# A gated causal convolution on one core: oct 0's eight direct tiles made as four pairs with a shared sum

## The chip, the cores and the metric

The kernel runs on one core of one Trainium2 chip. The time is the device time of one execution in microseconds (us); the profile's span lies inside it. The engines are TensorE (PE in the profile; its weight loads are PEld), VectorE (DVE), ScalarE (ACT), GpSimd (POOL) and the queue engine SyncE (SP), which issues nearly all DMAs.

## The reference

A dilated causal convolution over time, 15 taps at distance 2, with 144 channels in and 288 out, then a gate and a projection. All data are bf16; x is 2 x 16000 x 144.

```python
xp = jnp.pad(x, ((0, 0), (28, 0), (0, 0)))              # (K-1)*dil = 28
h = sum(einsum('btc,cd->btd', xp[:, 28-2*i : 28-2*i+T], w[i]) for i in range(15))
z = tanh(h[..., :144]) * sigmoid(h[..., 144:])
return z @ w_o
```

## The kernel before

**Tiles.** The 32000 time steps lie as 128 partitions of 250 consecutive steps. A tile is one position within these 250, on all 128 partitions: 128 rows that one matmul multiplies by a tap's weights. Eight positions make an oct; 250 = 2 + 31 x 8. The octs -4 to -1 hold the 28 steps of history and the two odd positions, oct 0 the first eight, and octs 1 to 30 the rest, handled in 15 pairs of octs. Of the 144 input channels the first 128 are transposed into XA (by channel), and the last 16 are gathered for eight taps at a time into XBc, copied to STB and transposed into XB. So the straightforward sum for a tile is 15 matmuls of XA with the taps WA and two of XB with WB. All these matmuls are recorded under one line (740, the helper `mm`), each 128x128 by 128x288.

**Direct tiles.** The first ten output positions, the two odd ones (k = 0, 1) and oct 0 (k = 2 to 9), are made in this straightforward way by `direct` (taps, in four pieces of weights as these arrive, the last first) and `direct_b` (the two of XB). Two tiles share a pair of PSUM banks, `dp`, and `finish` passes both through tanh and sigmoid (ACT, lines 761 and 764) and the product (DVE, line 769) into Z. In the planner they are floating: they have low priority and fill PE where nothing else can run.

**The loop.** From oct 1 on, a faster algorithm makes tiles in groups from sums of taps and differences of tiles. Its 30 units u = 0 to 29 (two for each pair of octs) run in steps t = -1 to 29. DVE makes the differences ahead (line 692): V and DU between tiles two and four apart, DD of V, and GX, GU, GV and GD between octs (`v_first`, `v_second`, `v_third`, `g_diffs`). Sums of weights (line 623, `wsum`) go to WS (neighbouring taps), WC, WT, WV and WD. PE forms parts of the results in PSUM: the items S0, S1, X0a to X1b, Y0a, Y0b, Y01, VE and VF. ACT copies a half-made bank to its neighbour (`copy`, line 898; 925 and 967 for whole pairs), and DVE adds the parts (lines 1019, 1031, 1040). The items D00 to D11 put the last matmuls in, and `finish` follows. O0 to O2 are projections: SP transposes Z into ZT, PE multiplies it by WOR (line 839), ACT copies PSUM to OS (line 847), SP stores it.

**Order.** A string in PATTERNS gives the order of the items for each t, with PATTERN where there is no entry. A + after an item means that it is done for the next unit. `stage(m)` prepares a pair of octs: load Xr, copy its 128 channels to STA and transpose to XA (`load_xa`), gather the others with `compact_chunk` into XBc, difference them (line 639), copy twice to STB (`load_xb`, line 672) and transpose to XB. `prepare(m)` makes the differences. SPREAD and SPREAS say at which step of two t's the ten pieces of `prepare` and the eight of `stage` may start: by a soft dependence on PE's last loop matmul before it.

**The planner.** Nothing of this is a fixed program order. `_Graph` records operations with what they read and write, a modelled duration and a priority, and `run` fills each engine's list: always the operation that can start first by the model, then the one of lower priority number, then the one recorded first. Combining, gates and copies in PSUM have 0, weight sums and evictions 1, differences 2, direct tiles 2. The two XB transposes by PE stand behind an empty `warm(0)`, which wants bank 6, in which oct 0's XA is transposed. The engines then run these lists in order, with semaphores between.

**The start.** Four loads of x (Xp) and four of weights (WA, last taps first) come in. PE warms up with 40 matmuls on ONES (line 548), transposes octs -4 to 0 (line 572), and DVE (oct -4) and ACT (the others, line 581) evict them to XA. ACT also compacts the 16 channels (line 541), and XB for octs -1 and 0 is transposed by PE (line 609) and evicted by ACT (line 613). The first loads through staging are those of octs 1 and 2. POOL loads WOR in 16 DMAs (line 1146), which wait until XB of oct 2 has landed (`xb2`).

Of the kernel before, what the change touches and what calls it, by code (L numbers as in the profile page):

```python
# [5 lines left out]
ACT = mybir.ActivationFunctionType  # L6
# [5 lines left out]
NP = 128  # L12
# [315 lines left out]
def _conv_wavenet_kernel(nc, x, w, w_o, out):  # L328
# [38 lines left out]
    KF = 0  # L367
    WARMS = 0
    LAG = 2
    PATTERNS = {29: 'O2 O1 Y01 Y0a D11 O0 Y0b D01 D00 D10', 28: 'Y0a X0a+ O1+ Y0b X0b+ O2+ D11 S0+ D10 X1a+ D00 Y01 S1+ X1b+ VE+ O0+ D01 VF+', 1: 'Y0a O2+ X0a+ Y0b X0b+ D11 X1a+ O1+ D00 S0+ D10 Y01 S1+ X1b+ D01 VE+ VF+ O0+', 0: 'Y0a X0a+ Y0b D11 X0b+ D00 X1a+ O2+ O1+ O0+ S0+ D10 Y01 S1+ X1b+ D01 VE+ VF+', 2: 'Y0a O2+ X0a+ O1+ Y0b X0b+ D11 D00 S0+ X1a+ D10 Y01 S1+ X1b+ D01 VE+ O0+ VF+'}  # L370
    EARLY = 4
    EARLYC = 1
    SPREAD = 12
    SPREAS = 9
    PATTERN = "Y0a O2+ X0a+ O1+ Y0b X0b+ D11 D00 S0+ X1a+ D10 Y01 S1+ X1b+ D01 VE+ VF+ O0+"

    with contextlib.ExitStack() as st:
        def sb(name, shape, dt):
            return st.enter_context(nc.sbuf_tensor(name, shape, dt))
# [5 lines left out]
        STB = sb("STB", [NP, NST, 12, 128], BF16)  # L385
        XA = sb("XA", [NP, NA, 8, 128], BF16)
        V = sb("V", [NP, NV, 2, 4, 128], BF16)
        DU = sb("DU", [NP, ND, 4, 128], BF16)
        DD = sb("DD", [NP, ND, 2, 4, 128], BF16)
        XB = sb("XB", [NP, NB, 12, 128], BF16)  # L390
# [50 lines left out]
        def aslot(o):  # L441
            return (o + 4) % NA
# [10 lines left out]
        def oct_of(e):  # L453
            return (e - E0) // 8, (e - E0) % 8
# [90 lines left out]

        def warm(n):
            bk = _Bank(BANK_O)
            g.add("pe", [lambda t: t.matmul(PS[:, BANK_O * 512:BANK_O * 512 + 128], lhsT=ID[:], rhs=ONES[:], start=True, stop=True)] * n,  # L548
                  r=["ID", "ONES"], alloc=[bk], frees=[bk], dur=0.07 * n)

        warm(40)
# [94 lines left out]
        def load_xa(o):  # L646
            s, q = aslot(o), o % NST
            ci = chunk_of(8 * o)
            i0 = 8 * o - CH[ci][0]
            src = Xr[:, ci % NX, i0:i0 + 8, 0:DA]  # L650
            if o <= EARLY:
                g.add("act", lambda a: a.activation(STA[:, q, :, :], src, ACT.Copy), r=[("Xr", ci % NX)], w=[("STA", q)], dur=0.92, prio=1, soft=gate[:1])
            else:
                g.add("dve", lambda v: v.tensor_copy(STA[:, q, :, :], src), r=[("Xr", ci % NX)], w=[("STA", q)], dur=0.335, prio=2, soft=gate[:1])
            g.add("sp", lambda e: e.dma_start_transpose(XA[:, s, :, :], STA[:, q, :, :].rearrange("p a b -> p (a b)")),
                  r=[("STA", q)], w=[("XA", s)], dur=1.3, dma="xa", nbytes=8 * 128 * 128 * 2)

        def load_xb(o, parts=(0, 1)):
            s, q = bslot(o), o % NST
            e0 = E0 + 8 * o  # L660
            ck = set()
            for e in range(e0 - 28, e0 + 8):
                if e >= EP:
                    ck.update([("XBc", chunk_of(e - E0)), ("XBd", chunk_of(e - E0))])
                else:
                    ck.update(hk5 + ["XBcz", "XBd_h"])
            m4 = (e0 + 2) // 4

            for h in parts:
                def cp(v, h=h):  # L670
                    src = bass.AP(XBc[:].tensor, (MB - 1 - m4 - h) * DB, [[8 * MB * DB, NP], [MB * DB, 6], [1, 128]])
                    return v.activation(STB[:, q, 6 * h:6 * h + 6, :], src, ACT.Copy)  # L672
                g.add("act", cp, r=sorted(ck, key=str), w=[("STB", q, h)], dur=0.708, prio=2 if gate else 0, soft=gate[:1])
            if 1 not in parts:
                return
            return g.add("sp", lambda e: e.dma_start_transpose(XB[:, s, :, :], STB[:, q, :, :].rearrange("p a b -> p (a b)")),
                  r=[("STB", q, 0), ("STB", q, 1)], w=[("XB", s)], dur=1.7, dma="xb", nbytes=12 * 128 * 128 * 2)
# [13 lines left out]
        def tt(dst, a, b, r, wk, n, prio=2):  # L691
            return g.add("dve", lambda v: v.tensor_tensor(dst, a, b, ALU.subtract), r=r, w=wk, dur=t_tt(n), prio=prio, soft=gate[:1])

        V0 = -3

        def v_first(o):
            s, p, q = aslot(o), aslot(o - 1), vslot(o)
            if o == V0:
                for f, pos in ((0, 6), (1, 2)):
                    tt(ap(V, 8 * q + 4 * f + 2, [2]), ap(XA, 8 * s + pos, [2]), ap(XA, 8 * s + 4, [2]), [("XA", s)], [("V", q, f)], 256)  # L700
                return
            ka = [("XA", s), ("XA", p)]
            if p == s - 1:
# [361 lines left out]
        def direct(k, b, pi, t0, t1, after=None):  # L1065
            e = H + k
            g.add("pe", region(b, [(lambda e_=e - DIL * i: xa_tile(e_)) for i in range(t0, t1)], [(lambda i_=i: WA[:, i_, :]) for i in range(t0, t1)], t0 == 12),
                  r=[("XA", aslot(o)) for o in sorted(set(oct_of(e - DIL * i)[0] for i in range(t0, t1)))] + [("WA", pi)], dur=(t1 - t0) * MM, floating=k >= KF, prio=2 if k >= KF else 1, soft=(after,), **({"alloc": [b.bk]} if t0 == 12 and k % 2 == 0 else {"w": [b.bk]}))

        def direct_b(k, b):  # L1070
            e = H + k
# [10 lines left out]
            return ((-1) % NZ, 6 + k) if k < 2 else (0, k - 2)  # L1082

        wa_order = [(3, wa_pieces[3]), (2, wa_pieces[2]), (1, wa_pieces[1]), (0, wa_pieces[0])]
        for pi, (t0, t1) in wa_order:
            for k in range(6):
                direct(k, db[k], pi, t0, t1)
        fin = []
        for k in range(6):
            direct_b(k, db[k])  # L1090
            if k % 2:
                fin.append(finish(dp[k // 2], zdir(k - 1), zdir(k)))

        def direct_parts(k):
            out = [lambda pi=pi, t0=t0, t1=t1: direct(k, db[k], pi, t0, t1, fin[0] if k >= 8 and t0 == 12 else xb_op if k == 6 and t0 == 12 else None) for pi, (t0, t1) in wa_order]

            def last():
                direct_b(k, db[k])
                if k % 2:
                    finish(dp[k // 2], zdir(k - 1), zdir(k))  # L1100
            return out + [last]

        for k in range(6, 10):
            for f in direct_parts(k):
                f()
        load_xa(1)
        compact_chunk(0)
        g.add("act", lambda a: a.activation(WC[:, 2, 3, :], WB[:, 1, :], ACT.Copy, scale=-1.0), r=[("WB", 1)], w=[("WB", 3)], dur=0.31, prio=2)
# [5 lines left out]
        for i in range(4):  # L1114
# [3 lines left out]
            else:  # L1118
                wsum(lambda: WC[:, 1, 3, :], lambda: WA[:, 12, :], lambda: WA[:, 14, :], [("WA", 3)], [("WC", 1, 3)], 0.25)
                wsum(lambda: WC[:, 0, 3, :], lambda: WC[:, 1, 3, :], lambda: WA[:, 13, :], [("WC", 1, 3), ("WA", 3)], [("WC", 0, 3)], 0.25)  # L1120
        for i in range(4):
            n = 2 if i < 3 else 1
            wsum(lambda i=i, n=n: WS[:, 2 * i:2 * i + n, :], lambda i=i, n=n: bass.AP(WA[:].tensor, 4 * i * N2, [[15 * N2, NP], [2 * N2, n], [1, N2]]),
                 lambda i=i, n=n: bass.AP(WA[:].tensor, (4 * i + 1) * N2, [[15 * N2, NP], [2 * N2, n], [1, N2]]), [("WA", i)], [("WS", i)], 0.4 if n == 2 else 0.25)
        wsum(lambda: WB[:, 2, :], lambda: WB[:, 0, :], lambda: WB[:, 1, :], [("WB", 0), ("WB", 1)], [("WB", 2)], 0.25)
        wsum(lambda: WT[:, 0:2, :], lambda: bass.AP(WC[:].tensor, 0, [[12 * N2, NP], [2 * N2, 2], [1, N2]]), lambda: bass.AP(WC[:].tensor, N2, [[12 * N2, NP], [2 * N2, 2], [1, N2]]),
             [("WC", 0, i) for i in range(4)], [("WT", 0), ("WT", 1)], 0.4)
# [4 lines left out]
        for h in range(2):  # L1132
            wsum(lambda h=h: WD[:, h, :, :], lambda h=h: WA[:, 8 * h:8 * h + 3, :], lambda h=h: WA[:, 8 * h + 4:8 * h + 7, :], wak, [("WD", h)], 0.52)
        wsum(lambda: WT[:, 5, :], lambda: WS[:, 5, :], lambda: WA[:, 14, :], [("WS", i) for i in range(4)] + [("WA", 3)], [("WT", 5)], 0.25)
        for o in range(-3, 1):
            v_first(o)
        for o in range(-2, 1):
            v_second(o)
        for o in range(-2, 1):
# [194 lines left out]
```

## Time and profile before

| | |
|---|---|
| median of 6 runs | 322.39 us (321.72 to 324.72) |
| profiled execution | 322.66 us, its span 320.9 us |
| PE busy, matmuls | 313.9 us, 2670 |
| DVE / ACT / POOL busy | 282.2 / 269.1 / 16.9 us |
| DMA | 50.40 MB, mean 157 GB/s |
| granted TensorE clock | 1.000 |

Stretches of the span, in us from its start. "Idle" is the stretch less the engine's busy time.

| stretch | what it is | PE busy | DVE busy | ACT busy |
|---|---|---|---|---|
| 0 to 8.9 | loads, warm-up, first XA | 6.83 | 1.84 | 3.21 |
| 8.9 to 16.3 | XA of octs -2 to 0, direct tiles | 7.37 | 6.56 | 5.53 |
| 16.3 to 24.9 | direct tiles; weight sums on DVE | 8.60 | 8.60 | 8.60 |
| 24.9 to 32.9 | t = -1, with direct tiles | 8.00 | 8.00 | 6.35 |
| 32.9 to 43.9 | t = 0, with the last direct tiles | 11.00 | 9.56 | 9.33 |
| 43.9 to 62.6 | t = 1 and 2 | 18.64 | 17.80 | 16.23 |
| 62.6 to 287.2 | t = 3 to 26, each 9.36 | 224.60 | 209.55 | 197.02 |
| 287.2 to 297.0 | t = 27 | 9.80 | 5.59 | 8.03 |
| 297.0 to 321.0 | t = 28, 29 and the rest | 19.05 | 14.70 | 14.85 |

How to read it: the page's first part gives each engine's busy time and share of the span. The chain that ended last goes back from the last instruction to what released it, so it names the work that set the end; in time order its columns are start, duration, engine and line. A row of the timeline has start, duration from first start to last end, engine, line, operation, tiles (out <- in), count, and in brackets the idle time before it with its releaser. An instruction's own duration has a tail that overlaps the next one, so the cost of one more instruction in a full engine is the distance between starts: matmuls last 286 ns each and start some 123 ns apart.

### The profile page before, as it was taken

Reading aid. Unit: us, or ns where it says so; the run is one execution under the profiler, and the core shown is the slowest. Engines: PE = TensorE matmul, PEld = TensorE weight load, DVE = VectorE, ACT = ScalarE, POOL = GpSimd, SP = SyncE. Lnnn points to the kernel's source line nnn. Section 1 sums busy time; section 2 is a strip of 40 time slices with the busy share of each in tenths; the row PEclk is TensorE's granted clock in tenths of the full one; section 3 lists DMA queues with packets and bytes.
Section 4 is the critical chain, followed back from the end, with each engine's and each line's share of the span. In section 5 each row is a group of like instructions: output and inputs, shape, how many; then the busy total and the mean of one; then the engine's idle time right before and its main releaser. Section 6 shows DMA issues by size and latency. Waiting matters only on the chain.

```text
span 320.9 us, 6963 instructions
## 1 busy us (share of the span) xinstructions
PE 313.9 (98%) x2670; PEld 244.1 (76%) x2670; DVE 282.2 (88%) x610; ACT 269.1 (84%) x636; POOL 16.9 (5%) x29
## 2 busy tenths in 40 slices
PE   7999999999999999999999999999999999999994
PEld 7787777777777777777777777777777777777674
DVE  1899989898998989899898989989898998884774
ACT  2798689889797988979798897979889797778674
POOL 8108100000000000000000000000000000000000
PEclk9999999999999999999999999999999999999999
DMA  8799994949589396969969499893969377131753
GB/s 207 213 219 186 233 217 99 195 111 202 153 144 243 76 236 108 179 176 102 243 119 235 109 196 158 134 254 73 181 167 191 90 142 172 47 68 72 112 128 96
DMA packets 127822, 50.40 MB, mean 157 GB/s; under 512 B 119134, under 2 KB 121615, under 8 KB 127789
## 3 DMA queue, kind: packets, MB, share of 16 engines
q1 hardware_dynamic: 127273, 49.62, 75.7%
q0 software_dynamic: 512, 0.33, 0.8%
q8 instruction: 21, 0.34, 0.4%
q14 instruction: 12, 0.10, 0.1%
q10 hardware_dynamic: 4, 0.01, 0.0%
HBM read 11.82 MB, written 9.22 MB: 66 GB/s over the span
## 4 chain that ended last, share of the span: by engine, by line
PE 96%; ACT 2%; DVE 1%; issue 0%; POOL 0%; ACTq 0%; POOLq 0%
PE PS L740 84%; PE PS L839 9%; PE PS L548 1%; PE PS L572 1%; ACT TS L761 0%; PE PS L870 0%; PE PS L797 0%; ACT PS L898 0%; ACT TS L764 0%; DVE WC L623 0%; ACT OS L847 0%; ACT OS L801 0%; PE PS L609 0%; PE PS L789 0%; ACT PS L925 0%
## 5 line engine op out<-in xcount | busy, mean ns | idle before, releaser
L1019 DVE TENSOR_TENSOR Xp<-PS,UX 128x576 f32<-128x576 f32 x90 | 62.8, 750 | 19.6 <-PE PS L740 19.3
L740 PE MATMUL PS<-WB,XB 128*128 128x288 bf16 x260 | 71.9, 286 | 0.0
L1031 DVE TENSOR_TENSOR PS<-PS,Xp 128x576 f32<-128x576 f32 x90 | 68.2, 757 | 2.1 <-ACT OS L847 1.0
L740 PE MATMUL PS<-WA,GD 128*128 128x288 bf16 x360 | 69.9, 286 | 0.0
L761 ACT ACTIVATE TS<-PS 128x288 f16<-128x288 f32 x125 | 51.5, 412 | 11.9 <-PE PS L740 10.8
L847 ACT ACTIVATE OS<-PS 128x432 bf16<-128x432 f32 (+1 forms) x88 | 42.3, 488 | 13.8 <-PE PS L839 12.8
L764 ACT ACTIVATE TS<-PS 128x288 f16<-128x288 f32 x125 | 51.5, 412 | 0.0
L672 ACT ACTIVATE STB<-XBc 128x768 bf16<-128x768 bf16 x60 | 50.7, 854 | 0.7 <-DMA XB<-STB 0.7
L898 ACT ACTIVATE PS<-PS 128x288 f32<-128x288 f32 x120 | 46.3, 408 | 2.6 <-PE PS L740 2.5
L967 ACT ACTIVATE UX<-PS 128x576 f32<-128x576 f32 x60 | 39.2, 653 | 10.4 <-PE PS L740 10.1
L740 PE MATMUL PS<-WS,GU 128*128 128x288 bf16 x210 | 44.3, 287 | 0.0
L839 PE MATMUL PS<-WOR,ZT 128*128 128x144 bf16 (+1 forms) x322 | 42.4, 253 | 0.0
L740 PEld LDWEIGHTS PS<-WA,GD 128*128 128x128 bf16 x360 | 34.6, 98 | 9.6 <-DVE PS L1031 0.8
L769 DVE TENSOR_TENSOR Z<-TS 128x288 bf16<-128x288 f16 x125 | 36.7, 298 | 4.3 <-ACT TS L764 4.0
L740 PE MATMUL PS<-WC,XB 128*128 128x288 bf16 x120 | 34.3, 286 | 0.0
L839 PEld LDWEIGHTS PS<-WOR,ZT 128*128 128x128 bf16 x322 | 27.9, 98 | 6.3 <-ACT OS L847 0.5
L740 PE MATMUL PS<-WD,DD 128*128 128x288 bf16 x180 | 31.9, 286 | 0.5 <-ACT PS L898 0.5
L740 PE MATMUL PS<-WC,V 128*128 128x288 bf16 x180 | 30.6, 286 | 0.0
L740 PE MATMUL PS<-WA,DD 128*128 128x288 bf16 x180 | 30.6, 286 | 0.0
L740 PEld LDWEIGHTS PS<-WB,XB 128*128 128x128 bf16 x260 | 25.4, 98 | 6.4
L740 PE MATMUL PS<-WT,DU 128*128 128x288 bf16 x120 | 24.5, 286 | 0.1
L740 PEld LDWEIGHTS PS<-WS,GU 128*128 128x128 bf16 x210 | 18.5, 98 | 7.5 <-ACT PS L898 0.3
(82 smaller groups left out, 469.3 us busy)
## 6 DMA issues: line engine op xcount, KB each, us to landing
Xr<-in_x_dram SPq DMA_DIRECT2D x15, 576.0 KB, 4.6
out_dram<-OS SPq DMA_DIRECT2D x30, 288.0 KB, 3.2
WA<-in_w_dram SPq DMA_DIRECT2D x3, 288.0 KB, 5.7
ZT<-Z SPq DMA_TRANSPOSE x32, 3.7
Xp<-in_x_dram SPq DMA_DIRECT2D x2, 252.0 KB, 5.8
XA<-STA SPq DMA_TRANSPOSE x30, 3.4
XB<-STB SPq DMA_TRANSPOSE x30, 5.0
Xp<-in_x_dram SPq DMA_DIRECT2D x1, 441.0 KB, 4.3
```

The source lines that it names most:

```text
L548: g.add("pe", [lambda t: t.matmul(PS[:, BANK_O * 512:BANK_O * 512 + 128], lhsT=ID[:], rhs=ONES[:], start=True, stop=True)] * n, r=["ID", " ...
L672: return v.activation(STB[:, q, 6 * h:6 * h + 6, :], src, ACT.Copy)
L740: return lambda t: t.matmul(bank(bk.b), lhsT=lhs(), rhs=rhs(), start=start, stop=True, skip_group_check=True)
L761: return a.activation(TS[:, s, 0, :, :], both(bk, 0, D), ACT.Tanh)
L764: return a.activation(TS[:, s, 1, :, :], both(bk, D, D), ACT.Sigmoid)
L769: return v.tensor_tensor(dst, TS[:, s, 0, :, :], TS[:, s, 1, :, :], ALU.mult)
L839: return t.matmul(PS[:, c0:c0 + n * D], lhsT=ZT[:, zt, blk, :], rhs=WOR[:, wi:wi + n, :].rearrange("p a b -> p (a b)"), start=first, stop= ...
L847: return e.tensor_copy(dst, src) if eng == "dve" else e.activation(dst, src, ACT.Copy)
L898: g.add("act", lambda e: e.activation(bank(bk.b + 1), bank(bk.b), ACT.Copy), w=[bk], dur=t_act(N2), prio=0)
L967: g.add("act", lambda e: e.activation(UX[:, k, u % NU, :, :], both(X, 0, N2), ACT.Copy), r=[X], w=[("UX", k, u % NU)], frees=[X], dur=t_ac ...
L1019: g.add("dve", lambda v, k=k, wi=wi, vb=vb, us=us: v.tensor_tensor(wslot(wi), both(vb, 0, N2), UX[:, k, us, :, :], ALU.add), r=[vb, ("UX", ...
L1031: return v.tensor_tensor(both(d, 0, N2), src, wslot(wi), ALU.add)
```

## The change

Oct 0's eight tiles are now made as four pairs. A pair is two positions two steps apart: a tile e with weights of all taps, and the tile e + 2. Written with neighbouring taps (2j, 2j+1), both tiles contain the same term, the sum of these two taps' weights (WS) times one tile of XA, and each has a remainder: a difference of two tiles two apart (V) times one of the two taps. So PE first makes the shared sum in the pair's first bank (`pair_sum`, eight matmuls), ACT copies it to the second bank, and then PE adds the remainders to both (`pair_own`, 15 matmuls for the two banks together), and the XB tail and `finish` as before (`pair_end`). The tiles k = 0 and 1 stay direct. Since the own matmuls add on to what ACT wrote, the second banks are written by a matmul first: `warm` goes over the odd banks with 12 of its 40 matmuls (128, 128 and 32 columns in each), and for the third pair, whose banks served the transposes, one extra matmul does it.

The differences V now begin one oct earlier: oct -3 gets the whole set and a small VX serves for oct -4. The sums WS and the first differences are recorded ahead of the direct tiles, not behind all weight sums. The sums of the first NQ0 = 2 pairs are mixed with the two direct tiles; the others come later.

The copies to STB for octs 3 and 4 (two each) go from ACT to DVE (BDVE); the copies to STA for octs 1 to 4 stay on ACT (AACT names the same octs as EARLY did). The compaction of chunk 1 goes from ACT to DVE (EARLYC 1 to 0). The patterns of t = 0, 1 and 2 are written anew, t = -1 and 27 get one of their own, and SPREAD goes from 12 to 10.

```diff
-    PATTERNS = {..., 1: 'Y0a O2+ X0a+ Y0b X0b+ D11 X1a+ O1+ D00 S0+ D10 Y01 S1+ X1b+ D01 VE+ VF+ O0+', 0: 'Y0a X0a+ Y0b D11 X0b+ D00 X1a+ O2+ O1+ O0+ S0+ D10 Y01 S1+ X1b+ D01 VE+ VF+', 2: 'Y0a O2+ X0a+ O1+ Y0b X0b+ D11 D00 S0+ X1a+ D10 Y01 S1+ X1b+ D01 VE+ O0+ VF+'}
-    EARLY = 4
-    EARLYC = 1
-    SPREAD = 12
+    PATTERNS = {..., 1: 'X0a+ Y0a O1+ O2+ Y0b X0b+ D11 X1a+ D00 S0+ O0+ X1b+ Y01 S1+ D10 D01 VE+ VF+', 0: 'Y0a X0a+ Y0b X0b+ D11 D00 S0+ D10 O2+ O1+ Y01 S1+ X1a+ D01 VE+ X1b+ VF+ O0+', 2: 'Y0a O0+ X0a+ O1+ Y0b X0b+ D11 D00 X1a+ S0+ D10 Y01 S1+ X1b+ D01 VE+ VF+ O2+', -1: 'X0a+ Y0a Y01 O2+ Y0b S0+ D11 D10 X0b+ O1+ X1a+ S1+ X1b+ D01 VE+ D00 O0+ VF+', 27: 'Y0a O2+ X0a+ O1+ Y0b X0b+ D11 D00 S0+ X1a+ D10 Y01 S1+ X1b+ D01 VE+ O0+ VF+'}
+    AACT = (1, 2, 3, 4)
+    BDVE = (3, 4)
+    EARLYC = 0
+    NQ0 = 2
+    NQD = 0
+    SPREAD = 10
     PATTERN = "Y0a O2+ X0a+ O1+ Y0b X0b+ D11 D00 S0+ X1a+ D10 Y01 S1+ X1b+ D01 VE+ VF+ O0+"
...
+        VX = sb("VX", [NP, 2, 128], BF16)
...
+            fns = [lambda t, c=512 * b + c, m=min(128, N2 - c), first=c == 0: t.matmul(PS[:, c:c + m], lhsT=ID[:], rhs=ONES[:, 0:m], start=first, ...)
+                   for b in (1, 3, 5, 7) for c in range(0, N2, 128)] if n else []
+            fns += [lambda t: t.matmul(PS[:, BANK_O * 512:BANK_O * 512 + 128], lhsT=ID[:], rhs=ONES[:], start=True, stop=True)] * max(0, n - 12)
...
-                g.add("act", cp, r=sorted(ck, key=str), w=[("STB", q, h)], dur=0.708, prio=2 if gate else 0, soft=gate[:1])
+                g.add("dve" if o in BDVE else "act", cp, r=sorted(ck, key=str), w=[("STB", q, h)], dur=0.27 if o in BDVE else 0.708, prio=2 if gate else 0, soft=gate[:1])
...
-        V0 = -3
+        V0 = -4
             if o == V0:
-                for f, pos in ((0, 6), (1, 2)):
-                    tt(ap(V, 8 * q + 4 * f + 2, [2]), ap(XA, 8 * s + pos, [2]), ap(XA, 8 * s + 4, [2]), [("XA", s)], [("V", q, f)], 256)
+                tt(ap(VX, 0, [2]), ap(XA, 8 * s + 6, [2]), ap(XA, 8 * s + 4, [2]), [("XA", s)], ["VX"], 256)
...
+        def pair_sum(q, pi, after=None):
+            n, r = QS[q]
+            bk = dp[q + 1]
+            es = [E0 + 4 * n + r - 4 * j for j in jset(pi)]
+            pre = [mm(_Half(bk, 1), lambda: ID[:], lambda: WA[:, 12, :], True)] if q == 2 and pi == 3 else []
+            g.add("pe", pre + region(_Half(bk, 0), [xa_tile(e) for e in es], [WS[:, j, :] if j < 7 else WA[:, 14, :] for j in jset(pi)], pi == 3), ...)
+            if pi == 0:
+                g.add("act", lambda e: e.activation(bank(bk.b + 1), bank(bk.b), ACT.Copy), w=[bk], dur=t_act(N2), prio=0)
...
+        def pair_own(q, pi):
+            for f in range(2):
+                for j in jset(pi):
+                    if 2 * j + f >= K:
+                        continue
+                    o, p = (n - j) // 2, (n - j) % 2
+                    fns.append(mm(_Half(bk, 1 - f), V[:, vslot(o), f, 2 * p + r, :] if o > -4 else VX[:, r, :], WA[:, 2 * j + f, :], False))
...
         for pi, (t0, t1) in wa_order:
-            for k in range(6):
+            for k in range(2):
                 direct(k, db[k], pi, t0, t1)
+            for q in range(NQ0):
+                pair_sum(q, pi, xb_op if q == 2 and pi == 3 else None)
...
+        for q in range(4):
+            if q >= NQ0:
+                for pi in range(3, -1, -1):
+                    pair_sum(q, pi, (xb_op if q == 2 else fin) if pi == 3 else None)
+            for pi in range(3, -1, -1):
+                pair_own(q, pi)
+            pair_end(q)
```

## The prediction

> **What bounds the kernel now.** I read the page first, then the chain that ended last in order of time, then windows by stage, then DVE, ACT and SP one instruction at a time up to 45 us. On the page, the shares and the chain:
>
> ```profile
> PE 313.9 (98%) x2670; PEld 244.1 (76%) x2670; DVE 282.2 (88%) x610; ACT 269.1 (84%) x636; POOL 16.9 (5%) x29
> ...
> PE 96%; ACT 2%; DVE 1%; issue 0%; POOL 0%; ACTq 0%; POOLq 0%
> ```
>
> PE is busy 98% of the span and carries 96% of the chain: a matmul that goes is worth its spacing, if PE has other work ready at that moment. The chain in time shows where that holds:
>
> ```profile
> 6.12 0.65 PE PS L572 x6
> ...
> 13.38 2.45 PE PS L740 x20
> 15.83 0.67 PE PS L609 x12
> 16.50 27.65 PE PS L740 x224
> ...
> 297.45 0.38 PE PS L839 x4
> 297.86 0.83 ACT OS L847 x2
> 298.69 0.31 ACT PS L898
> 299.05 2.39 PE PS L740 x18
> ```
>
> From 16.50 PE runs 224 matmuls without a break, 27.65 / 224 = 0.1234 us apart. At 297.86 the chain leaves PE for ACT: a copy that PE needs stands behind two evictions of the output. The windows by stage (busy of PE, PEld, DVE, ACT, POOL):
>
> ```profile
> 16.30:24.90 8.60, 8.60 (x74) 6.89 (x72) 8.60 (x26) 8.60 (x18) 0.00 (x0) 1.00 1.11 226
> 24.90:32.90 8.00, 8.00 (x67) 6.28 (x65) 8.00 (x19) 6.35 (x13) 7.81 (x15) 1.00 0.95 177
> ...
> 62.60:287.20 224.60, 224.60 (x1897) 174.29 (x1895) 209.55 (x443) 197.02 (x475) 0.00 (x0) 1.00 0.77 156
> ```
>
> From 16.3 to 32.9 DVE has no idle either. The direct tiles of oct 0 are what keeps PE busy there while DVE makes the differences: the change thins out the filler in the one stage where a second engine is full. From 62.6 to 287.2 PE has no gap and DVE 224.60 - 209.55 = 15.05 us idle. When DVE first gets free:
>
> ```profile
> 40.57 0.76 DVE L1031 TENSOR_TENSOR PS<-PS,Xp 128x576 f32<-128x576 f32 x1
> 41.24 0.29 DVE L769 TENSOR_TENSOR Z<-TS 128x288 bf16<-128x288 f16 x1
> 42.97 2.09 DVE L1019 TENSOR_TENSOR Xp<-PS,UX 128x576 f32<-128x576 f32 x3 [1.44 <-PE PS L740]
> ```
>
> **The change part by part.** One term each; a minus is a gain.
>
> Matmuls. Eight tiles took 15 tap matmuls each, 120. A pair takes 8 on the shared sum and 15 on differences: 4 x 23 = 92, and one that prepares a bank. The tail matmuls on XB (two a tile) stay. 120 - 93 = 27, at 0.1234: **-3.33 us**. The ends are this and 0 (all 27 fall into waits).
>
> Early shortage. Up to 16.50 the old PE did 50 tap matmuls, on six tiles. In the new order only the two remaining direct tiles (30) and the sums of the first two pairs (16) are open by then: differences accumulate on a copy of the finished sum, and this needs the last XA, which ACT delivered at 14.06 to 15.07. 50 - 46 = 4 matmuls of emptiness, **+0.49**. Lower end 0 (XA comes earlier, because fewer matmuls stand ahead of its transposes); upper end 1.5, if the XB tiles, evicted at 19.15 to 20.5 behind four STB copies, stay there: then only 22 own products are ready and 16.5 + 22 x 0.1234 = 19.2 leaves 1.3 us to 20.5. I take the lower region: XB's transposes find PE free earlier, and the STB copies need a compaction that ACT now does later.
>
> Copies of the sums. Four ACT copies of 128x288, mean 408 ns; own products wait for theirs. The wait is one copy and two hand-overs, some 0.6 us, twice side by side; four XB matmuls and the third pair's sum can stand in it. **+0.3**, between 0 and 1.0.
>
> DVE. Added: VX 0.20 (half of the two 256-wide differences at 9.31, next start 9.71); oct -3's whole difference instead of a part, 0.60 - 0.40 = 0.20; one compaction 0.15 (32.97 to 33.10, rounded up); four STB copies of 768, from the 1024-wide STA copy (34.63 to 34.97, 0.34), estimated 0.28 each, 1.12. Sum 1.67 us. The weight sums WS only move ahead. DVE has work to 41.45, so 43.1 now. PE would bring the wait at 42.97 forward by 3.33 - 0.49 - 0.3 = 2.54, to 40.4. DVE is short by 2.7. Of its queue two DD (0.60 each) and two GD (0.47) for octs 3 and 4, 2.14 us, are first read in t=2, after 53, and can slide behind. Left: **+0.5**; ends 0 and 2.7 (nothing slides).
>
> ACT. Four STB copies (16.22 to 19.15, 0.73 each) and a compaction (0.31) go, four copies (0.31 from start to start) come: 2.0 us less. 0: it is not on the chain before 297. But in the stretch before 20 ACT gets 1.5 of XB evictions, 0.6 of copies and 0.6 of gates ahead of the STB copies of octs 1 and 2, so their SP transposes issue up to 2.7 us later. Behind them wait POOL's 16 WOR loads, which began at 25.09 on that landing. They take 8.48 us and land 6.7 later at most: 40.3 before, 43.0 at worst after, against the first projection at 44.0 - 2.2 = 41.8. Cover 1.5 us; cost 0, at worst 1.2.
>
> [...] A copy on DVE, which the STB edit adds, has beside it the WOR issues of 502 to 710 ns on POOL, and the trace of before has no such copy within them until 32.97. [...]
>
> Pattern of t=27. The output group O0 now stands before VF, so its two evictions run beside VF's eight matmuls. PE stood from about 298.4 to 299.05; the copy could have begun at 298.36 instead of 298.58. **-0.2**; ends 0 and -0.65.
>
> The other patterns (t = -1 to 2) order the same items: 0, ends -0.5 (the waits of 0.2 at 44.24, 45.19 and 53.44 go) and +0.5. SPREAD 12 to 10 makes each pair of t's gate its ten preparations later, the last at step 33 of 36 and not 27, 3.1 us later; GD is read a whole t of 9.37 us afterwards. 0.
>
> Warm-up: 40 matmuls as before, four of them 32 columns wide and not 128. From 4.43 / 40 = 0.111 us this is up to 4 x 0.083 = 0.33 at 6.12. 0, because the next stage is paced by XA evictions and loads; lower end -0.33.
>
> **Sum**: -3.33 + 0.49 + 0.3 + 0.5 - 0.2 = -2.24 us. The profiled execution took 322.66 (span 320.9 and 1.76 around it): 320.4. It lies 0.27 above the median 322.39, so 320.15 on the median's level; I say 320.2.
>
> [...] The granted clock is 1.00 in every window, and PE's longest wait after its warm-up is about a microsecond, near 7 us. [...]
>
> **The rivals.**
> (a) DVE becomes the bound: nothing slides, so the hand-over at 42.97 comes at 43.1, and the saved matmuls turn into PE waiting on DVE between 30 and 44. For it: two windows with DVE 100% busy, and 1.67 us added there. Against: differences have the lowest priority in the planner, and combining PSUM the highest. Time 322.39 + 0.1 - 0.2 = 322.3.
> (b) The XB landing is late, and the first projection waits for WOR: 320.15 + 1.2 = 321.35. Against: the cover.
> (c) Slower: SPREAD 10. The mechanism is the steady loop, where DVE's preparations now pile up at the end of each pair of t's, against the next three PSUM additions. 24 t's are twelve pairs. A PE gap of 2.24 / 12 = 0.19 us a pair eats the gain; from 0.32 on it is slower by over 0.5%; with 0.4 it is 320.15 + 4.8 = 325.0. Against: 15.05 / 12 = 1.25 us of DVE idle a pair.
>
> **How the numbers follow.** Forecast 0.6, (a) 0.17, (b) 0.11, (c) 0.12. Half a per cent, 1.6 us, is about what a measurement of this kernel can tell from no change. The forecast's own range is 318.5 to 320.8: down by the least shortage, the whole of 0.65 at t=27 and some of the warm-up, up by half of DVE's upper end. Faster takes the forecast (0.6), same (a) and (b) (0.28), slower (c) (0.12). The range runs from 318.5 to 322.8, which takes in (a) and (b) and leaves out (c) and the tails.
>
> **What would show it.** Right: 2643 matmuls on PE; the third pair's sum and the first XB matmuls soon after 16 us; XB evicted before the STB copies; the loop's first group O near 41.8; PE without gaps from 62 on, a t still 9.37 us long. Wrong: PE waiting on DVE before Y0b, D11 or D00 between 28 and 44 (a); on ZT or WOR at the first projection (b); gaps that come back every 18.7 us (c); or PE empty between 19 and 21, with XB still behind STB.

## The result and the profile after

The changed kernel takes 321.44 us (median of 20 runs, 320.22 to 323.16); the kernel before, in the runs beside it and the earlier ones, 322.65 us (46 runs). The ratio is 0.9956, 95% interval 0.9943 to 0.9970: faster by 0.44%, or 1.4 us, and the whole interval lies below 1. The forecast was 320.2, a gain of 2.2 us. So the direction was right, the size between half and two thirds, and the gain stays just short of the half per cent that the prediction set as its limit for "faster". The time lies above the forecast's own range (318.5 to 320.8) and inside the wider one, which takes in the rivals. A repetition, told below, gave 0.9979 (0.9957 to 1.0000): the gain is known only as some 0.2 to 0.45%.

The profiled execution took 321.42 us, its span 319.5 against 320.9 before. The page's first part and the chain's shares by engine:

```profile
PE 310.9 (97%) x2643; PEld 239.1 (75%) x2643; DVE 284.5 (89%) x615; ACT 267.4 (84%) x635; POOL 16.9 (5%) x29
PE 89%; ACT 7%; DMA 2%; SPq 1%; issue 1%; ACTq 0%
```

There are 2643 matmuls, 27 fewer, and PE is busy 3.0 us less, close to the 3.33 expected. But the span fell by only 1.4, and PE's share of the chain fell from 96% to 89%, with 7% now on ACT. About half of what PE no longer does has become waiting. The chain in order of time (start, duration, engine, line) says where to look:

```profile
4.76 6.17 DMA Xp<-in_x_dram
...
15.06 1.40 ACT XB L620 x2
...
16.77 0.59 ACT PS L1111 x2
...
18.94 1.46 ACT STB L680 x2
...
24.01 0.31 ACT PS L1111
24.32 0.05 issue
24.36 14.30 PE PS L747 x114
...
41.74 0.84 ACT STB L680
42.58 0.59 ACT PS L905 x2
43.17 0.76 ACT STB L680
43.93 0.30 ACT OS L854
44.23 0.73 ACT STB L680
```

Two stretches that PE carried before belong to ACT: 13.1 to 24.3, from the last XA through XB, gates and the STB copies of octs 1 and 2 to the third pair's copy (L1111), and 41.7 to 46.8, where the STB copies of octs 5 and 6 stand between a copy in PSUM, an OS and a UX. Note that a chain names only the row that ended last; whether there is a second row just behind it must be tested, and here that is the main point.

To find where time is lost I set the same steps of the loop side by side. A step begins with its first matmul of the item Y0a; t=1 begins in the changed kernel with X0a+, 0.25 earlier (41.97).

| step begins at | t=0 | t=1 | t=2 | t=3 | t=28 | last ACT |
|---|---|---|---|---|---|---|
| before | 32.92 | 43.75 | 52.83 | 62.46 | 297.91 | 317.03 |
| after | 31.73 | 41.97 | 51.61 | 61.33 | 296.85 | 315.72 |
| gained so far | 1.19 | 1.78 | 1.22 | 1.13 | 1.06 | 1.31 |

Of 1.78 us gained by the start of t=1, 0.65 go in t=1 and 2. The long loop adds nothing (9.3658 us a step before, 9.3688 after, counted from t=3 to t=27) and the tail returns 0.25. The windows of exactly these two steps (length, then busy time of PE, PEld, DVE, ACT, POOL) in the kernel before:

```profile
43.75:52.83 9.08, 9.04 (x74) 6.34 (x72) 9.00 (x21) 7.56 (x19) 0.00 (x0) 1.00 0.78 171
52.83:62.46 9.63, 9.61 (x81) 7.18 (x79) 8.81 (x19) 8.81 (x21) 0.00 (x0) 1.00 1.00 142
```

and in the changed kernel:

```profile
41.97:51.61 9.64, 9.24 (x73) 6.48 (x71) 9.64 (x21) 9.38 (x22) 0.00 (x0) 1.00 0.83 156
51.61:61.33 9.72, 9.72 (x81) 7.14 (x79) 9.65 (x22) 8.62 (x21) 0.00 (x0) 1.00 1.06 196
```

PE's work is the same, 152 matmuls in the two steps. DVE has 0.64 us more in t=1 and 0.84 more in t=2. In t=2 it had 0.82 idle, and the step becomes 0.09 longer; in t=1 it had been full already (9.00 of 9.08), and the step becomes 0.56 longer. DVE's timeline in t=1 of the changed kernel shows what the additional work is:

```profile
44.26 0.77 DVE L1038 TENSOR_TENSOR PS<-PS,Xp 128x576 f32<-128x576 f32 x1
44.94 0.68 DVE L700 TENSOR_TENSOR DD<-V 128x1024 bf16<-128x1024 bf16 x1
45.53 0.76 DVE L1038 TENSOR_TENSOR PS<-PS,Xp 128x576 f32<-128x576 f32 x1
46.20 0.41 DVE L700 TENSOR_TENSOR GV<-V 128x512 bf16<-128x512 bf16 x1
46.53 0.55 DVE L700 TENSOR_TENSOR GD<-DD 128x768 bf16<-128x768 bf16 x1
47.00 0.30 DVE L776 TENSOR_TENSOR Z<-TS 128x288 bf16<-128x288 f16 x1
47.22 0.55 DVE L700 TENSOR_TENSOR GD<-DD 128x768 bf16<-128x768 bf16 x1
```

These are differences of octs 3 and 4, a DD, a GV and two GD, between the additions (L1038) that PE waits for: 1.86 us by the distance between starts. The kernel before made them in t=0, at 36.57 to 40.57. The prediction said that such differences "can slide behind". They did slide (one of the two DD stayed in t=0, the GV came along), and here they arrive. PE itself waits twice in t=1, once for each of the two suspects, DVE and ACT; in the kernel before, no wait in these steps is long enough to be marked:

```profile
42.85 0.41 PE L846 MATMUL PS<-WOR,ZT 128*128 128x144 bf16 x3 [0.23 <-DVE Xp L1026]
46.89 0.42 PE L747 MATMUL PS<-WT,XA 128*128 128x288 bf16 x2 [0.18 <-ACT TS L771]
```

### The profile page after: what moved, and what is told of

It reads as the page before. It is cut to its first block, busy times and chain, and to the rows that moved or that the text cites. A ratio compares the mean times of both kernels' runs of the same rounds, so it can differ in the third digit from the quotient of the medians.

```text
span 319.5 us, 6912 instructions
## 1 busy us (share of the span) xinstructions
PE 310.9 (97%) x2643; PEld 239.1 (75%) x2643; DVE 284.5 (89%) x615; ACT 267.4 (84%) x635; POOL 16.9 (5%) x29
## 4 chain that ended last, share of the span: by engine, by line
PE 89%; ACT 7%; DMA 2%; SPq 1%; issue 1%; ACTq 0%
PE PS L747 78%; PE PS L846 9%; DMA Xp<-in_x_dram 2%; ACT STB L680 2%; ACT STA L659 1%; ACT TS L768 1%; SPq L479 1%; ACT TS L771 1%; ACT PS L905 1%; ACT XB L620 0%; SPq L491 0%; PE PS L579 0%; PE PS L877 0%; ACT XA L588 0%; PE PS L804 0%
## 5 line engine op out<-in xcount | busy, mean ns | idle before, releaser
L1038 DVE TENSOR_TENSOR PS<-PS,Xp 128x576 f32<-128x576 f32 x90 | 68.2, 757 | 2.1 <-ACT OS L854 1.0
L768 ACT ACTIVATE TS<-PS 128x288 f16<-128x288 f32 x125 | 51.5, 412 | 13.1 <-PE PS L747 12.0
L680 ACT ACTIVATE STB<-XBc 128x768 bf16<-128x768 bf16 x56 | 47.6, 855 | 0.0
L747 PEld LDWEIGHTS PS<-WA,GD 128*128 128x128 bf16 x360 | 33.7, 98 | 11.2 <-DVE PS L1038 2.9
L747 PE MATMUL PS<-WA,V 128*128 128x288 bf16 x118 | 25.7, 286 | 0.3 <-ACT PS L1111 0.3
```

Source lines behind the costliest of these rows:

```text
L680: return v.tensor_copy(dst, src) if o in BDVE else v.activation(dst, src, ACT.Copy)
L747: return lambda t: t.matmul(bank(bk.b), lhsT=lhs(), rhs=rhs(), start=start, stop=True, skip_group_check=True)
L768: return a.activation(TS[:, s, 0, :, :], both(bk, 0, D), ACT.Tanh)
L1038: return v.tensor_tensor(both(d, 0, N2), src, wslot(wi), ALU.add)
```

## The experiments

Every timed kernel ran beside the kernel before on the same chip; a ratio is to that kernel, with its 95% interval. The reading to test: (1) early, up to 24 us, ACT's row and not PE ends last, so that saved matmuls are worth less there; (2) in t=1, DVE, fuller by what slid, holds PE, with ACT's row of late STB copies as a rival; and the other suspects SPREAD, the new patterns and the late load of Xr.

A caution on all of them: the planner makes its lists anew after an edit of a constant, so the order of any engine may change with it. Only the runs called "order kept" (e9, e10, e11) change a cost and nothing else. In two others, e1 and e12, the new lists have PE's order unchanged, which is used below.

| run | edit | ratio | interval | span |
|---|---|---|---|---|
| (changed kernel) | | 0.9956 | 0.9943 to 0.9970 | 319.5 |
| e5_after_again | none | 0.9979 | 0.9957 to 1.0000 | 319.4 |
| e1_spread12 | SPREAD 12 | 0.9992 | 0.9969 to 1.0015 | 319.5 |
| e2_stage_act | staging as before, with the pairs | 1.0086 | 1.0060 to 1.0112 | 324.0 |
| e6_stage_alone | staging as after, without the pairs | 1.0031 | 1.0017 to 1.0045 | 321.6 |
| e3_two_pairs_direct | two pairs direct | 0.9999 | 0.9977 to 1.0021 | 319.3 |
| e4_xr2_early | Xr loaded earlier | 1.0056 | 1.0034 to 1.0078 | 321.4 |
| e7_old_patterns | old patterns at t = -1 to 2 | 0.9998 | 0.9981 to 1.0014 | 320.7 |
| e8_no_27 | old pattern at t = 27 | 0.9987 | 0.9970 to 1.0004 | 320.6 |
| e9_short_stb56 | shorter ACT copies, octs 5, 6 | 0.9974 | 0.9955 to 0.9994 | 319.5 |
| e10_short_stb12 | shorter ACT copies, octs 1, 2 | 0.9954 | 0.9935 to 0.9973 | 319.2 |
| e11_narrow_own | 30 narrow matmuls | 1.0015 | 0.9990 to 1.0040 | 319.1 |
| e12_stb6_on_dve | oct 6's STB copies on DVE | 0.9949 | 0.9926 to 0.9972 | 320.1 |

The changed kernel measured twice gives 0.9956 and 0.9979 (medians 321.44 and 321.71), so differences under some 0.2% between these rows decide nothing.

**The loop: SPREAD.**

```diff
-    SPREAD = 10
+    SPREAD = 12
```

> The changed kernel with SPREAD back at 12. In the two traces a step t of the loop (t = 3 to 26) takes 9.367 us before and 9.373 to 9.377 after, and PE's weight loads wait for DVE's last additions 2.2 us in the loop instead of 0.6. Theory: SPREAD 10 pushes DVE's differences in front of these additions, so with 12 a t is 9.367 again and 0.2 us of the 321.44 come back (321.2). Rival: the loop's longer step comes from where DMAs and engines stand after the new start; then a t stays at 9.373 and the time at 321.44.

Measured 322.40 against 322.66. The step of the long loop is 9.3675 us with 12 and 9.3688 and 9.3700 in the two profiles with 10; over all runs here it lies between 9.366 and 9.374. So SPREAD costs nothing that can be told from that spread, and rival (c) is false. The setting does reorder the start, and nothing gets faster by going back.

**The two parts of the change, one at a time.** With the pairs (and with them the new patterns and SPREAD), but the staging copies as before:

```diff
-    BDVE = (3, 4)
-    EARLYC = 0
+    BDVE = ()
+    EARLYC = 1
```

> The changed kernel with the staging as before: the four STB copies of octs 3 and 4 and the compaction of chunk 1 back on ACT (BDVE empty, EARLYC 1). Theory: ACT, not DVE, is the fuller engine of the new start (the chain runs on ACT from 13.1 to 24.3), so 4 x 0.73 + 0.31 = 3.2 us more on ACT against 1.27 us less on DVE make it 0.5 to 1.5 us slower than the changed kernel (322 to 323). Rival, DVE as the bound of the start: 0.3 to 1.0 us faster (320.4 to 321.1).

Measured 325.56 against 322.66, 4 us worse than the changed kernel and far more than expected. In its chain, a landing of XA leads into a stretch that is mostly DVE's, up to 47:

```profile
26.99 5.30 DMA XA<-STA
...
32.65 0.75 DVE Xp L1026
...
34.40 0.33 DVE DU L700
...
41.17 1.20 DVE DD L700 x2
42.37 0.34 DVE GV L700
```

The pairs without the new staging are slower than the kernel before. The other half, made from the kernel before:

```diff
-    EARLYC = 1
+    EARLYC = 0
+    BDVE = (3, 4)
...
-                g.add("act", cp, ..., dur=0.708, ...)
+                g.add("dve" if o in BDVE else "act", cp, ..., dur=0.27 if o in BDVE else 0.708, ...)
```

> The kernel before with only the staging part of the change: the STB copies of octs 3 and 4 and the compaction of chunk 1 on DVE, the direct tiles as before. With the pairs, this part was worth 4.1 us (325.56 with it undone against 321.44). Theory: it is worth much only together with the pairs, since these make the start short of work and so dependent on ACT; with eight direct tiles PE has work up to 36 us, and ACT relieved by 3.2 us changes the end by less than 0.5 us (322.2 to 323.1). Rival: the staging part is the gain of the whole change and the pairs give nothing; then this kernel alone is 1 us or more faster than before (321.6 or less).

Measured 323.94 against 322.82, slower by 0.3%, which neither the theory nor the rival had. Its chain is PE until 33.1 and then DVE, at 33.1 to 36.4 and 46.1 to 54.3. So +0.9% and +0.3% alone, and -0.4% together: the parts do not add. Each alone was planned anew, so these are prices of whole plans and not of a copy; but in both, DVE's row is on the chain at the start of the loop.

**The early stretch: is PE the bound there?** The first two pairs made directly, 60 tap matmuls in place of 46:

```diff
-    NQD = 0
+    NQD = 2
```

> The changed kernel with NQD = 2: the first two of the four pairs are made as direct tiles again, so 2 x 7 = 14 of the 27 matmuls return. Theory: these matmuls run where PE had about a microsecond without work before 16.5, so they cost less than 14 x 0.1234 = 1.73: about 0.7 to 1.1 us (322.1 to 322.5). Rival: the holes before 16.5 stand on loads and stay as they are; then the whole 1.73 returns (323.2).

Measured 322.32 against 322.66, in the expected 322.1 to 322.5. By the profiles the 14 matmuls cost nothing: t=3 begins at 61.05, with 61.33 and 61.13 in the changed kernel. By the ratios they cost 0.2% to 0.43%, 0.6 to 1.4 us, of the 1.73 that they take on PE. The two do not agree; the interval lies above that of the first measurement and overlaps that of the repetition. That the saving of the first two pairs is only partly real fits both.

Then the same question with the order kept: the 30 own matmuls of these two pairs on 32 columns and not 288, so that PE has 2.9 us less to do by 24 us: from the first start to that of the next group the 15 of a pair take 0.39 and 0.38 us, and 1.84 each with 288 columns.

```diff
+                    c = 32 if q < 2 else N2
-                    fns.append(mm(_Half(bk, 1 - f), V[...], WA[:, 2 * j + f, :], False))
+                    fns.append(matmul(bank(b.b)[:, 0:c], lhsT=V[...], rhs=WA[:, k, 0:c], start=False, ...))
```

> The changed kernel, orders as they are, but the 30 own matmuls of the first two pairs are 32 columns wide and not 288 (the rest of their sums is left out). It takes about 30 x 0.09 = 2.7 us off PE between 17.1 and 21.3. Theory: PE is not what sets the start there, ACT is; the matmuls saved at that place are worth nothing, and the time falls by 0 to 0.5 us. Rival, PE is the bound from 16.5 on: t = 1 begins 2 to 2.7 us earlier.

PE's timeline shows that it uses none of this; it waits 3.25 us for the third pair's copy instead.

```profile
19.67 0.90 PE L747 MATMUL PS<-WS,XA 128*128 128x288 bf16 x6
23.82 1.03 PE L1124 MATMUL PS<-WA,V 128*128 128x288 bf16 x7 [3.25 <-ACT PS L1111]
```

The copy comes at 23.46, against 24.01 and 23.34 in the changed kernel's two profiles: it is on time with or without the matmuls. Of 2.9 us at most 0.45 reach t=1 (41.77 against 42.22 and 42.02 at Y0a). So between 17 and 24 us PE is not the bound. The timed runs had a surprise, told in the last section.

What is, by the chain, is ACT's row. With the order kept, the STB copies of octs 1 and 2 were cut from six blocks to one on ACT; POOL clears STB beforehand.

```diff
+        g.add("pool", lambda p: p.memset(STB[:]..., 0.0), ...)
...
-                    dst = STB[:, q, 6 * h:6 * h + 6, :]
+                n6 = 1 if o in (1, 2) else 6
...
+                    dst = STB[:, q, 6 * h:6 * h + n6, :]
```

> The changed kernel, orders as they are, with the four ACT copies to STB for octs 1 and 2 cut from six blocks to one (left out of the computation; POOL clears STB before they run, at about 8 to 10 us, where it has nothing else to do). It takes some 2.2 us off ACT between 18.8 and 22.5, in the stretch where the chain lies on ACT (13.1 to 24.3). Theory: ACT's row delays the XB transposes on SP, with them XA of oct 4, Xr chunk 2 and the STB copies of octs 5 and 6; so t = 1 begins 0.3 to 1.0 us earlier than 42.0, t = 1 and 2 lose less, and the time falls by 0.7 to 1.3 us. Rival, PE or DVE sets the start: under 0.2 us.

Measured 320.97 against 322.83, 0.7 below the repetition of the uncut kernel (321.71) and 0.5 below its first measurement; the intervals overlap, and in the profile t=1 comes only 0.2 to 0.4 earlier. Expected were 0.3 to 1.0 for t=1 and 0.7 to 1.3 for the time, so ACT's row is worth the lower end of that or less. ACT is gone from the chain between 14 and 28, and the next row stands right behind:

```profile
14.85 13.08 PE PS L750 x103
27.93 6.16 DMA XA<-STA
...
34.11 0.76 DVE V L703 x2
34.87 0.69 DVE PS L1041
```

XA of oct 4 lands at 34.1, and in DVE's fixed order the V that needs it stands ahead of an addition that does not. That landing was the second row in the repetition too.

**The repetition.**

> The changed kernel once more, on the same chip as the next three, so that parts can be compared within one set. Its ratio to the kernel before was 0.9956; expected again 0.994 to 0.998. In its trace t = 1 again begins about 42.0 and t = 3 about 61.3; if these move by more than 0.3 us with the same instruction order, it is the landing of the first loads that moves them.

No edit. Measured 321.71 against 322.82. The load of x on the chain landed at 10.27 and not 10.93, so everything up to 24 ran 0.66 earlier, and t=0 began at 31.06 (31.73 before). By t=1 0.2 of that was left, because XA of oct 4 landed at 34.27:

```profile
27.88 6.39 DMA XA<-STA
...
34.29 0.76 DVE V L700 x2
35.05 0.69 DVE PS L1038
```

So three rows end within half a microsecond of each other in this start: ACT's, the landing of XA of oct 4, and DVE. The first two are shown by e10 and by this profile; DVE's is read from the chains, and no run takes it away alone. This would be why none of the runs gains much.

**The load of Xr.** Its third chunk is issued at 33.26 and not at 26.54 as before, and with it come late the XBc and STB copies of octs 5 and 6, which stand on ACT at 41.7 to 46.2. Let it wait for an earlier event:

```diff
-                load_xchunk(nl[0]).deps.add(wa_op if nl[0] < 2 else xb2)
+                load_xchunk(nl[0]).deps.add(wa_op if nl[0] < 3 else xb2)
```

> The changed kernel with the load of Xr chunk 2 no longer held until XB of oct 2 has landed (the bound nl[0] < 2 becomes nl[0] < 3). In the trace after, that load was issued at 33.26 (26.54 before), the four STB copies of octs 5 and 6 then stand in one row on ACT from 41.7 to 46.2, on the chain, and t = 1 and 2 lose 0.65 us. Theory: with the load early the copies spread out, t = 1 and 2 lose at most 0.2, and the time falls by about 0.5 to 321.0. Rival, the new item order of t = 1 is what loses: no change of t = 1, 321.4. The earlier load may also take DMA time from XB of octs 1 and 2; then X0b of unit 0 waits before 28 and the time rises.

Measured 324.14 against 322.66: 2.7 us worse than the changed kernel, not better. t=0 begins at 33.08 and not 31.73. The chain from 22.7 to 36.4 now stays almost wholly on DVE, with a copy to STA at 31.64, of a kind that DVE first makes at 40.0 in the changed kernel. The earlier load brings DVE work into the stretch where DVE is full. So the early load does not pay in the plan that comes with it, against the expectation; what the late copies cost with the order kept is asked below (e9).

**The patterns.** Old order at t = -1 to 2, the new one at 27:

```diff
-    PATTERNS = {..., 1: 'X0a+ Y0a O1+ O2+ Y0b ...', 0: 'Y0a X0a+ Y0b X0b+ ...', 2: 'Y0a O0+ X0a+ ...', -1: 'X0a+ Y0a Y01 ...', 27: ...}
+    PATTERNS = {..., 1: 'Y0a O2+ X0a+ Y0b ...', 0: 'Y0a X0a+ Y0b D11 ...', 2: 'Y0a O2+ X0a+ ...', 27: ...}
```

> The changed kernel with the old patterns for t = -1 to 2 (t = 27 stays new). Theory: at t = 1 and 2 it is ACT's row of STB copies for octs 5 and 6 that costs 0.65 us, so with the old item order t = 1 and 2 lose the same, within 0.3, and the time stays within 0.4 us of the changed kernel. Rival: the new order of t = 1 is to blame, and the old one is 0.5 us faster. A third way: without their own order t = -1 and 0 wait for DVE's differences, and the time is 0.5 to 1.5 us above the changed kernel's.

Measured 322.53 against 322.82, 0.8 above the repetition, as the third way of the expectation had it; the two intervals overlap. Steps 1 and 2 take 19.44 us with the old order and 19.36 with the new, so the new order is not what costs there. The loss lies ahead of t=1, which begins at 43.01 (41.97 and 41.77 with the new order): PE waits 1.01 us at 35.54 behind DVE's additions, which stand in the chain from 32.0 to 35.5, and 0.40 at most at that place in the changed kernel's two profiles. So the new order of t = -1 and 0 seems to be a help, which the prediction had put at zero between -0.5 and +0.5.

Only the pattern of t=27 back to the old one:

```diff
-    PATTERNS = {..., 27: 'Y0a O2+ X0a+ O1+ Y0b X0b+ D11 D00 S0+ X1a+ D10 Y01 S1+ X1b+ D01 VE+ O0+ VF+'}
+    PATTERNS = {...}
```

> The changed kernel without a pattern of its own for t = 27. From the start of t = 28 to the last ACT instruction it took 19.08 us before and 18.83 after. Theory: without the pattern it is 19.08 again and the time rises by 0.25 us, with PE waiting again for a copy behind two evictions of OS. Rival: no difference from the pattern; then 18.83.

From t=28's first Y0a to ACT's last instruction 19.11 us, against 18.87 in the repetition: 0.24 for the pattern, as expected. Its chain has the two evictions of the output back, ahead of the copy:

```profile
297.62 0.83 ACT OS L854 x2
298.45 0.31 ACT PS L905
```

where the chain of the changed kernel has the copy alone:

```profile
296.04 1.24 PE PS L747 x10
...
297.30 0.40 ACT PS L905
```

The rest of this run's difference (t=3 at 62.10, not 61.13) arose before 45 us, where both have the same order: x landed at 10.97 and XA of oct 4 at 35.23. The start of this kernel varies by about a microsecond by such landings.

**Steps 1 and 2: ACT's late copies, or DVE?** With the order kept, the STB copies of octs 5 and 6 cut to one block each on ACT:

```diff
-                    dst = STB[:, q, 6 * h:6 * h + 6, :]
+                n6 = 1 if o in (5, 6) else 6
...
+                    dst = STB[:, q, 6 * h:6 * h + n6, :]
```

> The changed kernel, every engine's order as it is, but the four ACT copies to STB for octs 5 and 6 are one block of 128 long and not six (this part of the computation is left out). They stood in a row on ACT from 41.7 to 46.2 and on the chain. In the traces t = 1 and 2 together took 18.71 us before (43.75 to 62.46) and 19.36 after (41.97 to 61.33). Theory: these copies are what makes the difference, so t = 1 and 2 take 18.7 to 18.9, and the time falls by about 0.5 to 0.99 of the time before... as a ratio 0.995, against 0.9956 and 0.9979 for the changed kernel in its two sets. Rival, the new item order of t = 1: 19.3 as it was.

Measured 321.66 against 322.83, the same as the uncut kernel (321.71). From the first Y0a of t=1 to that of t=3 it takes 19.02 us, and 19.11 uncut. ACT has the time (its windows fall by 1.16 us between 42 and 53), and nothing comes of it. The chain goes over to the row behind:

```profile
41.88 1.42 DVE Xp L1028 x2
...
44.21 0.76 DVE PS L1040
44.97 0.59 DVE DD L702
45.56 0.68 DVE PS L1040
46.24 0.33 DVE GV L702
46.56 0.47 DVE GD L702
...
47.25 0.47 DVE GD L702
...
48.54 0.69 DVE PS L1040
```

PE's wait for ACT at 46.89 is gone, and one for DVE has come in its place:

```profile
49.27 0.42 PE L749 MATMUL PS<-WA,GD 128*128 128x288 bf16 x2 [0.23 <-DVE PS L1040]
```

So the ACT row, which the changed kernel's own chain names, is not what costs in t=1: the expected 18.7 to 18.9 us did not come. The time stayed where the rival had it, but the rival's reason, the new item order, does not fit e7. What is left is DVE, with the slid DD, GV and GD in it, 1.86 us of the 7.4 shown. No run takes work off DVE in t=1 with all orders kept. The nearest is e1 (SPREAD 12), where PE's order is the changed kernel's and DVE, in a new order, makes the second DD at 41.44 and not at 44.94, before t=1 and not in it: t=1 then takes 9.29 us, not 9.64, with DVE busy for all of it. (One STB copy of ACT also moved, and t=0 became longer, so that t=3 begins no earlier, at 61.35.) That fits DVE and is not a proof of it.

**A version that may be better.** Oct 6's two STB copies on DVE too:

```diff
-    BDVE = (3, 4)
+    BDVE = (3, 4, 6)
```

> A version that may beat both: the changed kernel with the STB copies of oct 6 on DVE as well (BDVE (3, 4, 6)); the planner makes the order anew. ACT gets 1.5 us less in t = 1, DVE 0.55 more. Theory: t = 1 and 2 take 0.3 to 0.6 us less than 19.36 and the ratio to the kernel before is 0.993 to 0.996. Rival: DVE has no room there either, as at 33 to 44 it is busy 10.86 of 11 us; then no change or slower.

Measured 321.34 against 322.83, ratio 0.9949 (0.9926 to 0.9972), the best ratio of all complete kernels. Counted as in e9, steps 1 and 2 take 18.77 us, 0.34 less than in the repetition, as expected, and PE carries the chain from 44.09 on. It is faster than the kernel before; that it beats the changed kernel is not shown, since the intervals overlap. Its profile does not show it either. By the traces every engine's order is the changed kernel's up to 44 us (but for two neighbours on DVE at 10.9), and PE's to the end; but XA of oct 4 landed at 35.27 here and t=1 began late, at 43.02 by Y0a, so DVE had caught up by then; t=3 begins at 61.79, later than in both profiles of the changed kernel. DVE still is full in the two steps (18.67 of 18.77 us).

That last relation holds in five plans: from the first matmul of step 1 or its Y0a to step 3, DVE was busy 17.81 of 18.71 us before, 19.29 of 19.36 after, 19.24 of 19.44 with the old patterns, 19.20 of 19.27 with the short ACT copies, and 18.67 of 18.77 here. Among these only the kernel before has DVE idle to speak of, and that in t=2. It is no general law: in e2, e3, e4 and e6 DVE was idle for 0.7 to 1.8 us of these steps, and e2 and e4 have the longest t=1 of all (10.33 and 10.00 us) with 1.2 us of DVE idle in it.

## Why the prediction was half right

- *Matmuls, -3.33.* 27 fewer, as counted, and 3.0 us less of PE busy time. But the price of 0.1234 each holds where PE has other work ready, and e11 shows a stretch (17 to 24 us) where it has not: 2.9 us less PE work gained at most 0.45.
- *Early shortage, +0.49.* Exactly 46 tap matmuls were done by 16.5. XB was evicted at 15.06 to 16.46, ahead of the STB copies, the first XB matmuls came at 16.52 and the third pair's sum at 21.8: all in the lower region, as chosen.
- *Copies of the sums, +0.3.* The first two cost nothing that shows. The third was waited for 0.33 us in the profile, as large as the term; but not for its own duration. It stands at the end of ACT's row.
- *DVE, +0.5: the step that failed.* The added work was sized well (the STB copies took 0.27 from start to start, estimated 0.28). By the start of t=1 the gain was 1.78 (1.98 in the repetition), against 3.33 - 0.49 - 0.3 - 0.5 = 2.04 by the sum; that much is right, though the wait for DVE itself shows only in the repetition (0.40 at 35.78). What failed is that 2.14 us of differences "can slide behind" for nothing because they are first read in t=2. A reader's due time says when work must be done; it does not say that there is room on the way. t=1 had 0.08 us of DVE idle in the profile of before, and t=2 0.82. DVE got 0.64 and 0.84 more, and the steps grew by 0.56 and 0.09: 0.65 us that the prediction put at zero. That the growth is there is measured five times (the two steps take 19.36 or 19.37 us in the changed kernel's two profiles and in e8, e10 and e11), and that ACT is not its cause is shown (e9); that DVE is its cause is read from the windows and the chain.
- *ACT, 0.* The delays were right: SP issued the XB of oct 2 at 20.43, 2.62 later (2.7 was the bound), and POOL's WOR loads began at 27.55 and not 25.09. The first projection ran at 42.85, held 0.23 by DVE and by no WOR, so rival (b) is false. What was not seen is that ACT's own row becomes the last to end from 13 to 24 us (e10: 0.2 to 0.7 us), and that late staging puts four STB copies into t=1. These, by e9, cost almost nothing behind DVE.
- *Pattern of t=27, -0.2.* Measured -0.24. *Other patterns, 0:* probably better than that; with the old ones the kernel was 0.8 us slower, with intervals that overlap. *SPREAD, 0:* right; the loop's step is 9.37 and PE without a gap from 62 on, so rival (c) is false. *Warm-up, 0:* the first tap came at 7.02 and not 7.78, and at 6.72 to 7.46 in all kernels with the new warm-up, 7.39 with the old one in e6; single profiles do not separate this from the landing of x.
- *Rival (a),* DVE the bound and nothing sliding, 322.3, had the right engine and the wrong place: the work slid as the forecast had it, and the bill came one step later. The result lies about midway between forecast and rival.
- *The STB copies on DVE beside POOL's WOR issues,* zero in the sum. Two of the copies ran within the issues, at 27.94 and 28.43. The first issue, with the copy of 27.94 inside it, took 0.88 us and 0.71 before; the other 15 took as long as before, so that the 16 took 8.64 us (8.48 before), and they landed a median of 4.4 us after issue (6.3 before). In the repetition the first issue took 0.71, and the two copies 0.40 each in place of 0.35. In e3, where all four copies ran among the issues, these took 9.08 us. So the 16 issues took 0.2 us longer than before in the changed kernel's first profile and 0.6 in e3's, well inside the cover of 1.5; that the copies are the cause is not shown.
- *Readings that were off,* without weight in the sum. PE's longest wait after the warm-up in the kernel before is 0.26 us, at 8.93, as far as t=28 (0.49 at 299.05), and not about a microsecond near 7. The clock column says 1.00 for the first microseconds too, but the transposes of 128 columns start 0.107 us apart until 7.30 and 0.055 from 9.31, with 1.00 in the windows 5.9 to 7.7 and 9.3 to 9.8 alike. DVE's last work before its wait at 42.97 ends at 41.53, not 41.45. The upper end of the shortage counts 22 own matmuls, but the first two pairs have 30. The terms named for the lower end of the forecast's own range lead to 318.9, not 318.5.

The sum as it came out: 1.78 by t=1, less 0.65 in t=1 and 2, less 0.07 in the loop, plus 0.25 in the tail: 1.31 at ACT's last instruction, and 1.4 in the span.

## What to carry to other kernels

Work that "can slide" is free only if the engine has idle time between its old place and its due time: take the window of each step on the way, and not the average of the loop, and pay for what does not fit. When a saving on the bounding engine is large against the idle time of the next ones, expect several rows to end together behind it; the chain then names only one of them, and shortening that one, with the order of everything else kept, tells whether it was the cost. In a kernel whose order comes from a planner, undoing half of a change may price another plan and not that half: compare the orders of the engines before comparing the times.

## What the runs showed of the hardware that was not expected

A kernel with less work took longer: 323.23 us, against 321.44 and 321.71 for the changed kernel. With 30 narrow matmuls (e11) the profiled execution had a span of 319.1 us at a granted clock of 0.999; the eleven executions after it had spans of 320.5 to 322.4 at a mean clock of 0.986 to 0.995, while the kernel before, beside it, had 0.994 to 1.000 in 34 of its 35 runs, and the three other kernels of that set (e9, e10, e12) 0.996 to 1.000. The lost clock and the longer span go together (0.995: 320.5 to 321.0; 0.986: 321.5 to 322.4). What is new in this kernel is the 30 narrow matmuls and the hole of 3.25 us on PE ahead of 23.82 that they leave; no run tells the two apart, and no profile of one of the slower executions exists, so what lowered the clock is not shown. In the changed kernel PE never waits longer than 0.4 us after its first 12 us.

The landings of loads and DMA transposes vary by nearly as much as the change is worth. In the six runs with the pairs and the new staging whose chain shows it, XA of oct 4 landed between 34.1 and 35.3 us: it was issued between 27.8 and 28.6 and landed 6.2 to 6.8 us later. The load of x on the chain landed between 10.2 and 11.0. Together they move the start of the loop by up to a microsecond, so that a single profile does not price an edit of half of one.
